# Another order for the opening of a fused state-space and MLP kernel: C's loads over two queues, later x and second weights, per-row products in place of wide ones

## The chip, the cores and the metric

The kernel runs on one core of a Trainium2 chip. The metric is the time of one execution in microseconds of the device; the kernel before took 336.55 us (median of three runs, 336.38 to 338.06). Engines are named as in the profile: PE (TensorE, its weight loads PEld), DVE (VectorE), ACT (ScalarE), POOL (GpSimd), SP (SyncE, which here only issues DMAs). ACT can issue DMAs too.

## The reference

A chunked state-space scan (Mamba-2) is followed by a two-layer MLP with a hard-swish in between. Inputs are x (4, 8, 768, 32), a (4, 8, 768), B and C (4, 8, 768, 16), and two weight matrices in float64, 256 x 2048 and 2048 x 256.

```python
log_a = np.log(np.clip(a, 1e-06, 1.0))
for c in range(nc):                          # chunks of 32 tokens
    cum = np.cumsum(la, axis=-1)
    L = np.exp(cum[:, :, :, None] - cum[:, :, None, :]) * causal
    CB = np.einsum('bhin,bhjn->bhij', Cc, Bc)
    y_intra = np.einsum('bhij,bhjd->bhid', CB * L, xc)
    y_inter = np.einsum('bhin,bhnd->bhid', Cc, state) * np.exp(cum)[:, :, :, None]
    y[:, :, sl] = y_intra + y_inter
    state = decay_full * state + np.sum(Bx, axis=2)
...
h = x @ w_in
g = h * np.clip(h + 3.0, 0.0, 6.0) / 6.0
return (g @ w_out).astype(np.float32)
```

## The kernel before

The kernel cuts the 768 tokens into NC = 6 chunks of P = 128 and each chunk into two halves of 64. The outer loop `for k in range(NC)` runs the MLP of chunk k while the scan of the next chunk is woven into it. Everything in front of that loop is the opening: it prepares constants, the scan of chunk 0 and part of chunk 1, and turns the first weights from float64 into float32. The order on every engine is the order in which the program writes the instructions (a manual schedule); the framework adds the waits.

The opening, in the names and lines that the change touches:

- Loads. `a` goes out on SP first (L83). `load_w(0, nc.scalar)` (L146) issues the first megabyte of weights on ACT, `load_bc(0)` issues C (as eight DMAs on SP, `pairs_first`, L99 to L106, one for each batch and parity of heads) and B (on ACT). `load_x(0)` and `load_w(1)` follow on SP. The activation table is loaded behind ACT's issues (L150).
- The decay matrix L. `log_a`, `add_up` (a scan) and `in_three` give the cumulative sums as three bfloat16 parts in `split`. PE builds the differences of every pair of tokens in PSUM: `diff_mask` (L355) writes the causal mask into eight banks, `mask_again` three of them once more, `diff_less` (L382) subtracts, `diff_pick` (L388) adds. `diff_pick` has two forms: 16 products of 64 columns for each batch with `pick`, or two wide ones with `of_batch` on rows that DVE has prepared in `spread_rows` (L277, two instructions). ACT takes the exponential (`diff_exp`, L404). `first_eto` (L409) makes the decay to each token.
- Products. `turn_b` transposes B on PE and copies it out of PSUM on ACT; `turn_squares` (L505) transposes C on DVE and `part_heads` (L511) splits it by head parity into `cT`. `scores` (L558) multiplies C and B into four banks `cb`, opens the banks of y (`own_banks`) and lets `into_state` (L581) multiply x with the decayed B (`ends`, on POOL). `multiply` (L608) copies the sums on ACT (`take`, L604, and two scalings to `mid`) and multiplies L with `cb` on DVE (L621). `mix` (L655) makes y from L and x (L667) and from the state (L545); `keep` (L676) copies y to `yT` on ACT, and `mlp_in` (L688) starts.
- Weights. `decode(i)` (L190) is a generator; `weights(i, n)` runs n of its steps. Its steps: a copy of the top 16 bits on ACT (L202) with the significand on DVE (L207, L211); exponent and sign masks on DVE (L221, L223); two relus on ACT (L227, L230); an OR and the last product on DVE (L234, L244). Three raw buffers hold the weights as loaded; `load_w(3)` uses the first again.
- Fillers. `diff_mask` contains 30 products of one column at its last batch of chunk 0 (L364), `busy` (L532) writes two products that nobody reads, and the last 18 of the 32 products of `mlp_in` are cut into two halves of 256 columns (L691).
- `renew(0)` (L638, DVE) makes the state after chunk 0, in `first_out`'s loop at (i, b) = (1, 0) (L1217).

The order of the opening is written out in L1137 to L1180.

## Time and profile before

| what | us |
| --- | --- |
| median of three runs | 336.55 |
| the profiled execution | 337.3 |
| its span | 335.6 |
| PE busy in the span | 327.6 |
| DVE, ACT, POOL busy | 264.2, 208.2, 130.3 |
| first product of `mlp_in` in the profile | 21.7 |

How to read it: the span is what the profiler covers, and the execution's own time has some more around it. A busy PE is not PE at its peak. A line of a timeline or chain gives the start in us from the span's start, the length, the engine, the line of the program and the operation, output before input. The chain of waits is followed back from the last instruction to whatever released each step; "issue" in it is time in which an engine waited for nothing that the profile shows.

## The change

Loads. The table load comes first on ACT. C's eight loads are cut by head, 32 partitions and four batches each, the even heads on ACT and the odd ones on SP. B and the first weights follow on SP. `load_x(0)` is called after the third `diff_exp` of chunk 0 and begins with a copy of one column into the tile on ACT, for which the DMA has to wait. `load_w(1)` is called behind the second step of `decode(0)` and begins with a memset on DVE.

Differences. `spread_rows`, `of_batch` and `of_head` go; every batch of both chunks takes the 16 products with `pick`. The masks are written by 18 products instead of 32; the 30 one-column products, `busy` and the halves in `mlp_in` go.

Order. C is turned and split right behind `in_three`. `turn_b(0)` copies on DVE for chunk 0. Chunk 1's batches 0 and 1 come ahead of the scores, 2 and 3 behind them; `own_banks` and `into_state` are calls of their own after the steps with the two relus. `renew(0)` moves up ahead of `mix(0)`. The second weights are decoded in one go by `decode_halves(1)` after `keep(0)`, with two halves of the columns in most of its steps.

```diff
@@ -98,6 +98,13 @@
 
         def pairs_first(src):
             t = loads.tile([P, 2, NB, 4, N], FP32, name="pairs", tag="bc")
+            if c == 0:
+                for h in range(NH):
+                    rows = slice(h // 2 * 32, h // 2 * 32 + 32)
+                    (nc.sync if h % 2 else nc.scalar).dma_start(
+                        out=t[rows, h % 2].rearrange("s b a n -> s b (a n)"),
+                        in_=src[:, h, sl, :].rearrange("b (s a) n -> s b (a n)", a=4))
+                return t
             for b in range(NB):
                 for h in range(2):
                     nc.sync.dma_start(
@@ -107,9 +114,11 @@
 
         if 0 < c < TURN:
             bcs[c] = [tokens_first(C, name="C", tag="bc")]
-        Bs[c] = tokens_first(B, nc.scalar if c == 0 else nc.sync, name="B", bufs=1)
         if c == 0:
-            bcs[c] = [pairs_first(C), Bs[c]]
+            bcs[c] = [pairs_first(C)]
+        Bs[c] = tokens_first(B, name="B", bufs=1)
+        if c == 0:
+            bcs[c].append(Bs[c])
         elif c < TURN:
             bcs[c].append(Bs[c])
         else:
@@ -118,6 +127,8 @@
     def load_x(c):
         sl = slice(c * P, (c + 1) * P)
         xts[c] = loads.tile([P, NB * NH, D], FP32, name="xt", bufs=1)
+        if c == 0:
+            nc.scalar.copy(out=xts[c][:, 0, :1], in_=bias_hi)
         nc.sync.dma_start(out=xts[c], in_=x[:, :, sl, :].rearrange("b h s d -> s (b h) d"))
 
     NP = 4
@@ -139,15 +150,13 @@
             src = moe_w_out[r0:r0 + FP * P, :].rearrange("(k p) m -> p k m", p=P)
             dst = raw.rearrange("p (k m) -> p k m", k=FP)
         raws[i] = raw
-        if i == 2:
+        if 0 < i < 3:
             nc.vector.memset(raw[:, :1], 0)
         queue.dma_start(out=dst, in_=src)
 
-    load_w(0, nc.scalar)
+    nc.scalar.preload_act_table_set("natural_log_exp_and_others")
     load_bc(0)
-    load_x(0)
-    load_w(1)
-    nc.scalar.preload_act_table_set("natural_log_exp_and_others")
+    load_w(0)
 
 
     ident = const.tile([P, P], FP32, name="ident")
@@ -187,6 +196,40 @@
         fill=0.0, base=N - 1, channel_multiplier=-1)
     parity = const.tile([P, 2], FP32, name="parity")
 
+    def decode_halves(i):
+
+        n, cut = NK * FP * P, FP * P // 2
+        top = raws[i].bitcast(U16).rearrange("p (k f w) -> p k f w", k=NK, w=4)[..., 3]
+        lo, hi = (raws[i].rearrange("p (n w) -> p n w", w=2)[:, :, w] for w in range(2))
+        s = att.tile([P, n], U16, name="ws").rearrange("p (k f) -> p k f", k=NK)
+        e = att.tile([P, n], U16, name="we").rearrange("p (k f) -> p k f", k=NK)
+        m = att.tile([P, n], U32, name="wm")
+        halves = [slice(h * cut, (h + 1) * cut) for h in range(2)]
+        for h in halves:
+            nc.scalar.copy(out=s[:, :, h], in_=top[:, :, h])
+        nc.vector.tensor_scalar(
+            out=m, in0=hi, scalar1=0xFFFFF, scalar2=0x100000,
+            op0=ALU.bitwise_and, op1=ALU.bitwise_or)
+        for h in halves:
+            for t, mask in ((e, 0x7FF0), (s, 0x8000)):
+                nc.vector.tensor_scalar(
+                    out=t[:, :, h], in0=s[:, :, h], scalar1=mask, scalar2=None,
+                    op0=ALU.bitwise_and)
+            nc.scalar.activation(
+                e[:, :, h].bitcast(BF16), e[:, :, h], AF.Relu, bias=bias_hi, scale=-8.0)
+            nc.scalar.activation(
+                e[:, :, h], e[:, :, h].bitcast(BF16), AF.Relu, bias=bias_lo, scale=-1.0)
+        nc.vector.scalar_tensor_tensor(
+            out=m.bitcast(FP32), in0=lo, scalar=2.0 ** -32, in1=m, op0=ALU.mult, op1=ALU.add)
+        load_w(i + NRAW)
+        m = m.bitcast(FP32).rearrange("p (k f) -> p k f", k=NK)
+        for h in halves:
+            nc.vector.tensor_tensor(
+                out=e[:, :, h], in0=e[:, :, h], in1=s[:, :, h], op=ALU.bitwise_or)
+            nc.vector.scalar_tensor_tensor(
+                out=w_in[i][:, :, h], in0=m[:, :, h], scalar=2.0 ** -20,
+                in1=e[:, :, h].bitcast(BF16), op0=ALU.mult, op1=ALU.mult)
+
     def decode(i):
 
 
@@ -198,10 +241,7 @@
         s = att.tile([P, n], U16, name="ws")
         e = att.tile([P, n], U16, name="we")
         m = att.tile([P, n], U32, name="wm")
-        for sl in (slice(0, n),) if i != 1 else (slice(0, n // 2), slice(n // 2, n)):
-            nc.scalar.copy(out=s[:, sl], in_=top[:, sl])
-            if i == 1 and sl.start == 0:
-                yield
+        nc.scalar.copy(out=s, in_=top)
 
         def significand():
             nc.vector.tensor_scalar(
@@ -222,13 +262,14 @@
             out=e, in0=s, scalar1=0x7FF0, scalar2=None, op0=ALU.bitwise_and)
         nc.vector.tensor_scalar(
             out=s, in0=s, scalar1=0x8000, scalar2=None, op0=ALU.bitwise_and)
-        next(parts_m, None)
+        if i:
+            next(parts_m)
         yield
         nc.scalar.activation(e.bitcast(BF16), e, AF.Relu, bias=bias_hi, scale=-8.0)
         next(parts_m, None)
         yield
         nc.scalar.activation(e, e.bitcast(BF16), AF.Relu, bias=bias_lo, scale=-1.0)
-        if i and i + NRAW < 2 * NP:
+        if i > 1 and i + NRAW < 2 * NP:
             load_w(i + NRAW)
         yield
         nc.vector.tensor_tensor(out=e, in0=e, in1=s, op=ALU.bitwise_or)
@@ -252,9 +293,6 @@
     picks = const.tile([P, G * N], BF16, name="picks")
     mid = pre[:G, 9].bitcast(BF16)[:, :2 * P]
     low = pre[:G, 10, :2 * P]
-    spread = [pre[:, 11 + c].bitcast(BF16).rearrange("k (h i) -> k h i", h=NH) for c in range(2)]
-    of_batch = const.tile([P, NB], BF16, name="of_batch")
-    of_head = const.tile([P, NH], BF16, name="of_head")
 
     cum_c = cum.rearrange("g (c p) -> g c p", p=P)
     ends_at = (slice(0, 2 * P), slice(2 * P, S))
@@ -264,21 +302,11 @@
             nc.vector.tensor_reduce(
                 out=pick, in_=ident[:, :pad].rearrange("g (r q) -> g q r", r=3), axis=AX.X,
                 op=ALU.add)
-            nc.vector.tensor_reduce(
-                out=of_batch, in_=pick.rearrange("k (b h) -> k b h", b=NB), axis=AX.X, op=ALU.add)
-            nc.vector.tensor_reduce(
-                out=of_head, in_=pick.rearrange("k (b h) -> k h b", b=NB), axis=AX.X, op=ALU.add)
         nc.scalar.mul(less, pick, -1.0)
         nc.gpsimd.tensor_copy(
             picks.rearrange("k (g n) -> k g n", n=N), pick.unsqueeze(2).to_broadcast([P, G, N]))
         nc.vector.tensor_reduce(
             out=parity, in_=head.rearrange("p q t -> p t q"), axis=AX.X, op=ALU.add)
-
-    def spread_rows(c):
-
-        nc.vector.tensor_tensor(
-            out=spread[c], in0=split[:, c].unsqueeze(1).to_broadcast([P, NH, P]),
-            in1=of_head.unsqueeze(2).to_broadcast([P, NH, P]), op=ALU.mult)
 
     def log_a(sl):
         nc.vector.tensor_scalar(
@@ -360,12 +388,7 @@
             d = ps_o.tile([P, NH, HT], FP32, name="d", tag="o")
         else:
             d = ps_y.tile([P, NH, HT], FP32, name="d", tag=f"y{b % 2}")
-        if (c, b) == (0, NB - 1):
-            for _ in range(30):
-                nc.tensor.matmul(
-                    out=d[:1, 0, :1], lhsT=ident_h[:, :1], rhs=hide[:, :1], start=True, stop=True,
-                    skip_group_check=True)
-        n = NH // 4
+        n = NH if c else NH // (2 if b == 0 else 4)
         for h in range(0, NH, n):
             nc.tensor.matmul(
                 out=d[:, h:h + n], lhsT=ident_h,
@@ -386,13 +409,6 @@
             start=False, stop=True, skip_group_check=True)
 
     def diff_pick(c, b):
-        if c or b >= 2:
-            for a, rows in enumerate(HALF):
-                nc.tensor.matmul(
-                    out=ds[c, b][rows], lhsT=of_batch[:, b:b + 1].to_broadcast([P, HT]),
-                    rhs=spread[c][:, :, rows], start=False, stop=True,
-                    tile_position=(0, a * HT), skip_group_check=True)
-            return
         for h in range(NH):
             for a, rows in enumerate(HALF):
                 g = b * NH + h
@@ -470,7 +486,7 @@
 
         t_ps = turn_ps(c, 1)
         transposes(c, 1, t_ps)
-        nc.scalar.copy(out=turned(c)[0], in_=t_ps)
+        (nc.scalar.copy if c else nc.vector.tensor_copy)(out=turned(c)[0], in_=t_ps)
 
     def turn_c(c, t_ps):
 
@@ -529,13 +545,6 @@
         part_heads(c)
         fade(c)
 
-    def busy(n, bank):
-
-        for _ in range(n):
-            nc.tensor.matmul(
-                out=bank[:, :256], lhsT=ident,
-                rhs=ident.unsqueeze(1).to_broadcast([P, 2, P]), start=True, stop=True)
-
     def from_state(c, a, pairs=range(NQ)):
 
         csT, state = bTs[c][2], (mids[c] if a else states[c - 1])
@@ -563,7 +572,7 @@
 
         bT, cT, _ = bTs[c]
         cbs[c] = [ps.tile([P, NB, 2, HT], FP32, name="cb", tag=f"f{q}") for q in range(NQ)]
-        if c not in ys:
+        if c not in ys and c:
             own_banks(c)
         for b in range(NB):
             for a, rows in enumerate(HALF):
@@ -575,7 +584,7 @@
                         tile_position=(32 * q, a * HT), skip_group_check=True)
         if c == TURN:
             from_state(c, 0)
-        if c <= TURN:
+        if 0 < c <= TURN:
             into_state(c, *range(1 if c == TURN else 2))
 
     def into_state(c, *halves):
@@ -688,7 +697,7 @@
     def mlp_in(k, f, between):
         h = ps.tile([P, TB], FP32, name="h", tag=f"f{f % 4}")
         for j in range(NK):
-            n = TB // (1 + (f * NK + j >= NF * NK - 18))
+            n = TB // (1 + (f * NK + j >= NF * NK - 0))
             for t in range(0, TB, n):
                 nc.tensor.matmul(
                     out=h[:, t:t + n], lhsT=w_in[f // FP][:, j, f % FP * P:(f % FP + 1) * P],
@@ -1144,38 +1153,40 @@
     in_three()
     for b in range(3):
         mask_again(0, b)
-    for c in range(2):
-        spread_rows(c)
-    diff(0, 0, 1)
-    diff(0, 2, 3)
-    weights(0, 1)
+    turn_squares(bcs[0][0], turned(0)[2])
+    part_heads(0)
+    for b in (0, 2):
+        diff(0, b, b + 1)
     for b in range(NB):
         diff_exp(0, b)
+        if b == 2:
+            load_x(0)
     first_eto()
-    diff(1, 2, 3)
+    turn_b(0)
+    diff(1, 0)
+    diff(1, 1)
     weights(0, 1)
     for b in range(NB):
         ends(0, b)
-    turn_b(0)
-    diff(1, 0, 1)
+    weights(0, 1)
+    load_w(1)
+    scores(0)
+    for b in range(2, NB):
+        diff(1, b)
+        diff_exp(1, b)
     weights(0, 2)
-    diff_exp(1, 2)
-    diff_exp(1, 3)
-    turn_squares(bcs[0][0], turned(0)[2])
-    part_heads(0)
+    own_banks(0)
+    into_state(0, 0, 1)
+    multiply(0)
     fade(0, HALF[1])
     weights(0, 1)
-    busy(2, ps.tile([P, NB * P], FP32, name="d", tag="f3"))
-    scores(0)
-    multiply(0)
+    weights(0, 1)
     load_w(2)
     load_w(3)
-    weights(0, 1)
-    weights(1, 1)
+    renew(0)
     mix(0)
-    keep(0, lambda: weights(1, 1))
-    weights(1, 3)
-    weights(1, 1)
+    keep(0)
+    decode_halves(1)
     load_bc(1)
     load_x(1)
 
@@ -1214,8 +1225,6 @@
                     first_out(b, i, c)
                     for n in w_more.get((i, b), ()):
                         next(ins[n])
-                    if (i, b) == (1, 0):
-                        renew(0)
                     if (i, b) == (1, 1):
                         by_token(cum_q)
                     if (i, b) == (2, 0):
```

## What I predicted, before the changed kernel had run

> **What bounds the kernel now.** I read the page first (busy times and slices), then the chain of waits of the first 50 us, then the timelines of PE, ACT and DVE before 24 us, then stretches of 1 us for the DMA.

> ```profile
> PE 327.6 (98%) x3361; PEld 272.8 (81%) x3361; DVE 264.2 (79%) x418; ACT 208.2 (62%) x448; POOL 130.3 (39%) x125
> ...
> 9.18 3.62 DMA pairs<-in_C_dram
> ...
> 12.98 1.12 DVE csT L507
> 14.13 0.89 DVE cT L517 x2
> 15.16 1.20 PE cb L572 x59
> 16.36 0.84 PE y L590 x50
> ...
> 17.22 0.38 ACT adds L606
> ...
> 17.64 0.90 PE y L667 x55
> 18.55 0.61 PE y L545 x16
> 19.16 0.26 PE y L667 x12
> 19.42 1.03 issue
> 20.44 0.75 PE y L667 x43
> 21.19 0.61 PE y L545 x16
> 21.80 27.75 PE h L693 x100
> ```

> The first line is the page's, the others are the chain: start, length, what. From 21.80 the chain is almost only TensorE, and over 49.5 to 335.6 PE is busy 282.4 of 286.1 us. So the change is worth what it does to the moment at which `mlp_in` starts (21.80). Before it the chain is: C's last load lands at 12.80, C is turned (L507), split by head parity (L517), multiplied with B (L572), the sums taken by ACT (L606), the mixing products (L667, L545), and in their midst PE stands 1.03 us for "issue", that is for nothing but its own instructions. From L667's start to `mlp_in` it is 21.80 - 17.64 = 4.16 us, 3.13 without that stall.

> ```profile
> 6.42 1.49 PE L378 MATMUL d<-hide,ident_h 128*128 128x512 bf16 x3
> 7.70 1.06 PE L383 MATMUL d<-less,split 128*128 128x512 bf16 x2
> 8.69 0.84 PE L399 MATMUL d<-split,pick 128*64 128x64 bf16 x32
> ...
> 12.93 1.15 ACT L227 ACTIVATE we<-we,bias_hi 128x1024 bf16<-128x1024 uint16 x1
> 14.11 1.15 ACT L230 ACTIVATE we<-we,bias_lo 128x1024 uint16<-128x1024 bf16 x1
> 15.17 1.07 ACT L407 ACTIVATE L<-d 128x512 f32<-128x512 f32 x2
> ```

> Timeline: start, length, instruction. PE takes 0.43 to 0.5 us for 512 columns up to about 8.6, then 0.026 us for 64 (32 in 0.84), twice as fast. ACT does its two relus of the first weights (2.3 us) in the shade of C's wait; that is the place to watch.

> **The profile's own time** is 337.3 us (span 335.6 and 1.7 around it), 0.75 over the median 336.55. I carry the change of `mlp_in`'s start to both.

> **Part 1, loads.** C was eight issues on SP, 1.25 to 9.75, held up in between (0.56 to 2.14 each). Now four go on SP and four on ACT, behind the table load (1.28, so 0.79 to 2.07). An issue costs ACT 0.47 to 0.49 by its own rows, up to 0.71 by SP's C rows: 1.9 to 2.8, I take 2.4. ACT is free at 4.5, not 3.08. Queued behind that are `less` (0.23) and the first logarithm, which started at 4.34: now about 4.7. DVE's scan and `in_three` wait for it, so `split` is whole at 7.5 instead of 7.23 (bounds 7.23 to 8.0).
> C lands between the last issue (4.5) + 2.6, the earliest C landing after its issue ended (a's: 1.19 to 3.8), and 4.5 + 3.62 = 8.1 by the chain's last C row. I take 7.5; DVE can use it from 7.5, and it costs nothing up to 10, since DVE then idles until 12.0.
> B follows on SP at about 4.0. Its packets took from 5.8 to 10.7 in the DMA records beside C's; a later B (issued 198.7) was down at 205. So it lands between 8 and 10.7, wanted at 11.1: nothing. The first weights, 6.0 us from issue to ACT's copy before, now come behind B: 10.7 to 13.4, wanted at 12.3. Even 13.4 only delays DVE's decode, which has 1 us in hand.

> **Part 2, TensorE and the first exponentials.** The masks are 18 instructions with the same 4096 columns, the 30 one-column products go, so PE is done with masks at about 6.9 and waits for `split`. `less` twice from 7.7 (1.06 by L383's row), picks from 8.69, as before, since PE itself held this back before. First exponential 9.3 (9.32). Batches 2 and 3 now have 32 picks (0.84) where four wide products took 0.62, so the four exponentials end at 11.75 plus the little copy that holds x (0.1 to 0.23): 11.9 against 11.53. In return DVE loses `spread_rows` (2.36) and two reductions (0.39), which is what lets it turn C at 7.5 to 8.7 and split it by 9.6.
> PE: `e_ps` at 10.85 (0.29), transposes of B to 11.75, DVE's new copy of `bT` 12.0 to 12.65 (0.59 by ACT's row, 0.68 by DVE's L621). PE next does chunk 1, batches 0 and 1 with picks, (0.22 + 0.42) x 2, to 13.05, then the scores, 1.2, to 14.25: 2.1 us earlier than before.

> **Part 3, what comes then on ACT.** After `eto` (to 12.3) and the copy of the sign halves (1.11, to 13.4) ACT's next instructions are the two exponentials of chunk 1, for which PE must first do another 0.65 each behind the scores: 15.2 to 16.3. Then the two relus, now uncovered, 1.17 each with their step: 18.65. Only behind them, in ACT's order, stands `take` (L606): 18.65 to 19.0. So L667 starts at 19.05 instead of 17.64. The two `mid` scalings (0.63) end at 19.65, before PE wants them (19.9).
> x is issued behind the third exponential, at 11.4 instead of 9.79. It took until 15.5 (5.7) before, 4.7 to 5.2 at 197.8 and 248.3: it lands at 16.1 to 17.1. The state products may start at 16.3, take 0.85, and are wanted at 18.6: up to 17.7 hidden.
> DVE: `wm` 12.65, then 0.69 + 1.23 + 0.64 + 0.52 to 15.7, L621's four (2.48) to 18.2, `fade` 0.42, the last two steps 0.68 + 1.22 to 20.6. All ahead of PE.

> **Sum.** L667 at 19.05 + 3.13 = 22.2 without the stall, 21.8 before: +0.4. The 1.03 gained is more than paid for by the 1.4 that ACT's relus cost.
> The stall: PE's instructions come in 16 KB pieces (26 pieces in the page's queue line); one piece ran at 18.50 for 0.97 us, just as the second weights' packets ended, and PE went on at 20.44. In the changed order that point lies in the first mixing half, the piece is asked for near 14.8, and the second weights, now issued behind DVE's sign step (15.7, 10.62 before), don't move before 17. I take no stall; 1.03 is the other end.

> **Part 4, second weights and after.** They land at about 20.0 (before: 18.7). ACT begins their copy when `keep` is done (22.5), and two halves of copy and relus (0.66 x 2, 0.6 x 4) end at 26.4; DVE finishes `w_in[1]` at 27.7 and the first `times_ramp` at 28.4. The fifth block reuses that bank at 22.2 + 6.87 = 29.1: hidden by 0.7 (1.7 before). If that is gone, each us late is a us on the path. `renew` (about 1 us of DVE) moves into the same stretch and is in these times; where it stood PE had no wait. Whole instead of halved products in `mlp_in`: 36 x 0.4295 against 72 x 0.2158, -0.1. PE's instructions up to its end are 517 either way (417 + 100, 453 + 64), so later pieces fall as before. Total +0.3 to +0.4.

> [...]

> **Rivals.** [...]
> [...]
> *The instruction stall stays* (another transfer stands before the piece): +1.0, **338.0**.
> *The loads don't do what they say:* C lands at 12.8 as before. Turning, splitting and the copy of `bT` are in DVE's order, scores start at 15.5, +2.5 more, **339.4**. Against: no weights run ahead of it now.
> *Faster by over 1.7:* L667 would have to start before 17.0, with the exponentials ending at 14.3; no row gives this.

> **Chances.** Forecast 0.34, earlier doubling 0.12, stall 0.12 (half of it beyond 338.2), slow PE 0.28, late loads 0.04, faster for a reason not seen here 0.10. A measurement of this kernel can tell about 0.5%, 1.7 us, from no change: same 0.34 + 0.12 + 0.06 = 0.52, slower 0.28 + 0.06 + 0.04 = 0.38, faster 0.10. Time 336.55 + 0.35 = 336.9. The likeliest case alone spans 336.2 to 337.9; with the others 335.3 to 339.0.

> **What would show it.** Right: L507 starts near 7.5, L572 near 13, L606 directly behind L230 near 18.6, L667 near 19, L693 near 22.2 and no "issue" between. Wrong: ACT's issues or L286 far later than 4.7; L399 at 0.05 us each after 8.7; L590 released by x's DMA after 17.7; waits of L693 for L801 or `w_in` between 28 and 36; L606 well ahead of L230.

## The result, and the profile after

| | before | after |
| --- | --- | --- |
| median of the runs side by side (us) | 336.98 (4 runs, 336.38 to 338.06) | 342.05 (4 runs, 341.87 to 342.62) |
| the profiled execution, its span | 337.3, 335.6 | 341.9, 340.2 |
| mean granted TensorE clock in the span | 1.000 | 0.983 |
| first mixing product (L667 / L676) | 17.64 | 17.30 |
| "issue" stall in the mixing | 1.03 | 3.10 |
| `mlp_in` begins, and its first stretch takes | 21.80, 27.75 | 24.83, 29.43 |

The change makes the kernel slower: ratio 1.015, 95% interval 1.0118 to 1.0181, outside the predicted range of 335.3 to 339.0. In what follows a ratio leaves out executions that stand over 1.5% above the fastest of the same kernel; where executions of one kernel fall into two groups, their single times are given.

The page of the changed kernel, its first line of busy times and the clock in 40 slices of 8.5 us:

```profile
PE 329.0 (97%) x3361; PEld 266.0 (78%) x3361; DVE 262.4 (77%) x420; ACT 208.5 (61%) x450; POOL 128.7 (38%) x125
...
PEclk9958999999999999999999999999999999999999
```

PE has the same 3361 products and is busy 1.4 us more. The new thing is in the second line: in the third slice, 17.0 to 25.5 us, TensorE was granted half its clock, after it had had the full one. The prediction has no term for that.

The chain of waits of the changed kernel (start, length, what):

```profile
16.99 0.27 ACT adds L615
17.25 0.04 issue
17.30 0.79 PE y L676 x49
18.09 3.10 issue
21.18 0.44 PE y L676 x8
21.62 1.04 PE y L554 x16
22.67 1.11 PE y L676 x61
23.78 1.04 PE y L554 x16
24.83 29.43 PE h L702 x64
```

Three things are to be seen. Mixing begins at 17.30, which is 0.34 *earlier* than before. After 56 products (49 of them on the chain) PE stops for 3.10 us with no wait that the profile shows ("issue"). And what follows is slow: L554's sixteen products take 1.04 us where before they took 0.61.

The stretches of 1 us of the changed kernel (stretch, its length, then each engine's busy share, granted clock, DMA share, GB/s):

```profile
16.00:17.00 1.00, 0.57 (x58) 0.41 (x34) 1.00 (x3) 1.00 (x2) 0.00 (x0) 1.00 0.89 209
17.00:18.00 1.00, 0.70 (x56) 0.63 (x57) 0.96 (x3) 0.77 (x3) 0.00 (x0) 1.00 0.91 377
18.00:19.00 1.00, 0.09 (x8) 0.00 (x0) 1.00 (x1) 0.00 (x0) 0.00 (x0) 0.55 0.90 360
19.00:20.00 1.00, 0.00 (x0) 0.00 (x0) 0.96 (x5) 0.00 (x0) 0.00 (x0) 0.50 0.10 41
...
28.00:29.00 1.00, 1.00 (x3) 0.39 (x2) 0.96 (x3) 0.97 (x2) 0.00 (x0) 0.83 0.05 16
```

The clock falls at 18.10, as the stall begins, and is back at 28.34. Its records have it full from 7.86 for 10.24 us, half for 10.24 and full again for 310.61; in the kernel before it is full from 9.07 for 327.68. These are 3, 3, 91 and 96 times 3.413 us, so stretches of 3.41 us are compared below. While PE has nothing to do, DMA is nine tenths busy until 19: these are the second weights' packets (15.57 to 19.39). In this window a piece of the queue that the page calls `instruction` moves (26 pieces, 0.43 MB, 16 KB each), seen in the DMA queues of 18.8 to 19.8 us:

```profile
q1 hardware_dynamic: 30, 0.07, 18.6%
q8 instruction: 1, 0.02, 5.9%
```

In the records this piece runs from 18.84 to 19.79, among the last of the weights' packets, and PE goes on at 21.18. In the kernel before it ran from 18.19 to 19.16 and PE went on at 20.44. That it carries instructions of PE is an estimate from these times: both stops end 1.28 and 1.39 us behind it. The piece is only 0.65 us later than before; but PE now comes to the place where it stops, taken here as the border between two pieces, at 18.09 instead of 19.42. There it had done 64 + 16 + 12 = 92 mixing products, here 56, as the timelines count them (the chain lists fewer, since not every product stands on it). 36 more of its products stand ahead of `mlp_in` (453 against 417), so the border, behind the 349th product of PE's program in both kernels, has moved up the mixing by those 36, and the piece has not moved with it. Of the 2.07 us that the stall grew, 1.33 are the earlier border and 0.74 the later going on.

**Where 4.7 us come from.** Mixing starts 0.34 earlier; the stall is 3.10 - 1.03 = 2.07 longer; the rest of the mixing takes 24.83 - 17.30 - 3.10 = 4.43 instead of 3.13, 1.30 more; `mlp_in` up to the next long chain piece takes 29.43 instead of 27.75, 1.68 more. The last agrees with 3.5 us (24.83 to 28.34) at half clock. -0.34 + 2.07 + 1.30 + 1.68 = +4.71; the span grew by 4.6. Behind 54 us the difference stays between 4.5 and 4.7. So 2.07 is the stall and about 3 the clock, and the opening that the change rearranged gives back 0.34.

The opening itself, from the timeline of the changed kernel (start, length, engine, instruction, in brackets the idle time before it and what ended it):

```profile
0.79 1.28 ACT L157 ACT_TABLE_LOAD   x1 [0.79 <-PEq L1380]
0.82 2.71 ACTq L104 DMA_DIRECT2D pairs<-in_C_dram  x4
...
6.61 1.08 DVE L523 STREAM_TRANSPOSE csT<-pairs 128x512 f32<-128x512 f32 x1
8.26 1.76 ACT L423 ACTIVATE L<-d 128x512 f32<-128x512 f32 x3 [3.63 <-PE d L415]
11.54 1.21 PE L581 MATMUL cb<-cT,bT 32*64 32x128 f32 x64
14.66 1.14 ACT L268 ACTIVATE we<-we,bias_hi 128x1024 bf16<-128x1024 uint16 x1
15.73 0.85 PE L599 MATMUL y<-xt,bs 64*32 64x64 f32 x64 [1.60 <-DMA xt<-in_x_dram]
15.84 1.15 ACT L271 ACTIVATE we<-we,bias_lo 128x1024 uint16<-128x1024 bf16 x1
16.89 0.35 ACT L615 COPY adds<-y 128x256 f32<-128x256 f32 x1
```

C is turned at 6.61, 6.4 us earlier than before, and the scores follow 3.6 us earlier; then L615 stands behind the two relus, and all but 0.34 of it is gone.

## The experiments

The profile leaves two readings open. **Packets:** the instruction piece waits behind the second weights' packets, and the stall, with it the slow clock, comes from that. **Clock:** the rearranged opening leaves PE too little work between 14 and 17 us (in the changed kernel PE is idle from 14.13 to 15.73), and the clock falls for that, stall or no stall. The runs set the one against the other, under names of their own: theories A, B and C, later R and M, are spelled out in the texts that stand before each result. A third reading, that ACT's sums come too late behind the relus, is set aside by the result, since the mixing begins earlier than before.

### Second weights behind the L times cb products

```
     multiply(0)
+    load_w(1)     # was ahead of scores(0)
```

> The changed kernel with one call moved: the second weights are loaded behind the four L times cb products on DVE (issue near 17 instead of 14.6 us). Theory A (two causes: the piece of PE's instructions is asked for near 15.8 and stands behind the second weights' packets, which gives the 3.1 us stall; and the clock is halved at 18.3 because of the thin PE work of the 3.4 us before it, whatever the stall does): the stall in the mixing products is gone, the clock still falls near 18.3, mlp_in starts near 21.5 and is some 1.5 us longer than 27.8; time 338 to 339.5. Theory B (one cause: the stall, which also cools the clock): no stall and the clock full throughout, mlp_in starts near 20.5; time 335.5 to 336.5. Theory C (the stall comes from the number of instructions and not from the transfer): still 3 us, time 341.5 to 342.5.

Measured: 340.57 us, ratio 1.0104 (1.0088 to 1.012). Theory A has the clock right and the stall wrong; B and C have neither. The chain of waits:

```profile
16.89 1.12 PE y L676 x54
18.01 1.66 issue
19.67 0.44 PE y L676 x8
...
23.31 29.45 PE h L702 x64
```

and its stretches, first the 3.41 us that end where the clock falls, then single us:

```profile
13.22:16.63 3.41, 1.25 (x80) 0.92 (x72) 3.38 (x7) 3.14 (x5) 0.00 (x0) 1.00 0.31 28
...
15.00:16.00 1.00, 0.42 (x42) 0.45 (x46) 1.00 (x3) 0.97 (x2) 0.00 (x0) 1.00 0.01 2
16.00:17.00 1.00, 0.54 (x47) 0.38 (x45) 1.00 (x4) 1.00 (x4) 0.00 (x0) 0.81 0.00 0
17.00:18.00 1.00, 1.00 (x56) 0.77 (x57) 0.96 (x3) 0.37 (x2) 0.00 (x0) 0.50 0.17 29
18.00:19.00 1.00, 0.01 (x1) 0.00 (x0) 1.00 (x1) 0.00 (x0) 0.00 (x0) 0.50 0.79 143
```

and the first of these stretches in the kernel before:

```profile
13.22:16.63 3.41, 2.70 (x103) 1.99 (x102) 3.00 (x6) 2.98 (x4) 0.01 (x1) 1.00 1.16 202
```

These rows tell the two apart. DMA is idle from 15 to 17, nothing stands before the piece (17.28 to 18.22 in the records; the weights' packets begin at 17.97), and the stall is 1.66 us instead of 3.10: that 1.4 goes to the packets. But the stall doesn't vanish, so the piece also begins late by itself. And the clock falls at 16.63, 1.4 us *before* PE stops: here the stall can't be what lowers it. In the 3.41 us before the fall PE was busy for 1.25, in the same stretch of the kernel before for 2.70. From 16.63 to 26.87 the granted clock is 0.50.

### Second weights with x

```
         if b == 2:
             load_x(0)
+            load_w(1)
```

> The changed kernel with the second weights issued directly behind x (near 10.6 instead of 14.6 us), so that their packets end some 1.5 us earlier (near 17.5 instead of 19.1). Theory A and B: PE goes on about 2.1 us after the last of those packets, as in both kernels so far (18.3 to 20.44, 19.1 to 21.18), so the stall shrinks from 3.1 to about 1.5; A has the clock fall near 18.3 all the same, time 339.5 to 341; B lets it stay full if the pause is short enough, time 337.5 to 338.5. Theory C: stall and time unchanged, 341.5 to 342.5.

Measured: 342.09 us, ratio 1.0144 (1.0114 to 1.0175), above what theories A and B had; C has the time but not the stall, which did shrink. The weights' packets run 14.61 to 18.42, as early as before the change (14.49 to 18.30), the piece comes at 17.95 among the last of them, and the stall is 2.17. So giving the weights their old time gives back only 0.9 of the stall, and again the clock falls first (17.30, stall at 17.95). PE goes on at 20.12, even 0.3 ahead of the kernel before; the stall is longer than its 1.03 because PE is at the border 1.5 us sooner.

### Filler products where PE was idle

```
+    zero = const.tile([P, P], BF16, name="zero")     # memset to 0
+    for _ in range(7):                               # ahead of weights(0, 2)
+        nc.tensor.matmul(out=cbs[0][3]..., lhsT=zero, rhs=ident_h..., start=False, ...)
```

> The changed kernel with seven products of a zero tile (512 columns each, added to the fourth cb bank) on PE between the last differences and the state products, where it waits 1.6 us for x. Second weights as in the changed kernel. Theory A: the clock doesn't fall near 18.3, since that window is now filled; the stall stays near 3 us and may itself cool the clock one window later, near 21.7; time 339 to 341.5, the lower end if it stays full. Theory B: stall and clock as in the changed kernel, 341.5 to 342.5. The state products start at most 0.2 us later than before.

Measured: 336.67, 343.78, 336.77 and 344.39 us, with a mean clock of 1.000 in the two short ones and about 0.985 in the others; before, 337.14 in the same set. Neither theory had the short ones (339 to 342.5). The chain of the profiled, short execution:

```profile
17.17 0.86 PE y L678 x53
18.03 0.61 PE y L556 x16
18.64 0.79 PE y L678 x53
19.43 0.61 PE y L556 x16
20.04 27.66 PE h L704 x64
```

No stall, full clock, and the mixing takes 2.87 us where `e1_w1_late` took 6.42 with a stall of 1.66 in it: 4.76, or 1.9 for the clock alone. The instruction piece now came at 14.70 to 15.75, ahead of the weights (15.38 on). So both losses are gone at once, and the run doesn't tell by itself which of them brings the other. What it does show is that seven products of no use are worth 5.2 us against the changed kernel, when they work. The two long executions were not profiled; that they miss the race between piece and packets is likely from `e12_m13_w1first_fill`, not shown. An estimate speaks for it: their mean clock is that of the changed kernel, where the slow clock cost about 3 us, and they are 7 us longer than the short ones, so about 4 are left for a stall.

It shows a second thing. `mlp_in` begins 1.76 earlier than in the kernel before, yet the span is only 0.6 shorter (335.0 against 335.6): 1.85 ahead at the end of `mlp_in` (47.70 against 49.55), 1.45 at 126, 0.6 at the end. The gain goes in parts: about 0.45 between 82 and 105 us, where the chain leaves PE for ACT and DVE at the splitting of weights (87 to 94.5) and the kernel before had PE alone, and about 0.3 near 176 and 0.4 near 223 us, at each of which the chain of `e3_fill` has a short "issue" (0.14 and 0.38).

### Both

> The fill of the run before and the late second weights together. Theory A: neither stall nor slow clock, mixing products at 17.3, mlp_in near 20.5 and 27.7 us long; time 335 to 336, that is 1 us under the kernel before. Theory B: the same as the late second weights alone. Theory C: 341 to 342.5.

With late weights and the filler: 340.98 us (338.68 to 341.88), ratio 1.0101 (1.0061 to 1.0141); theory A's 335 to 336 missed. With no weights in the way the piece still came only at 16.74, the stall was 1.63, and the clock fell at 19.71, 1.9 *after* the stall had begun this time. The filler thus keeps the clock up to the stall, but does not by itself bring the piece early; that it came at 14.70 in `e3_fill` and at 16.74 here, with the same products on PE, has no explanation in these runs. One difference is seen: at the border before this one PE had to stop for 0.23 us here (at 13.38), and not in `e3_fill`.

### The kernel before without its two products that nobody reads

```
-            busy(2, ...)
```

> The kernel before without its two products that nobody reads (busy, at 13.3 to 14.4 us). Theory A, now from the late second weights' run, where the clock was halved 1.1 us ahead of the stall: the clock falls where the PE work of some 3.4 us is thin. Without them PE works some 1.6 of the 3.4 us around 12.8 to 16.2, as in the changed kernel around 15 to 18.4, so the clock is halved for a part of the opening in most runs, mlp_in takes 1 to 2 us more and the time is 338.5 to 341. Theory B (only a stall cools it): no change, 336.5 to 338.

Measured: 337.28 us over ten runs, ratio 1.0014 (0.9995 to 1.0034). Theory A, by which the clock is halved for a part of the opening in most runs, missed: nine of the ten had a mean clock of 0.994 to 1.000, and one, of 340.04 us, 0.984. In the profiled execution, of 337.14, the clock was full and the stall 0.54 at 19.63, though PE was busy for only 1.68 of the 3.42 us from 13.17 to 16.59. So the two products of `busy`, which the change drops, are not what holds the clock in most executions of the kernel before. The thirty one-column products, which it drops too, were not taken out of that kernel by any run.

### The changed kernel with twenty one-column products

```
+        if (c, b) == (0, NB - 1):
+            for _ in range(20):
+                nc.tensor.matmul(out=d[:1, 0, :1], lhsT=ident_h[:, :1], rhs=hide[:, :1], ...)
```

> The changed kernel with 20 products of one column behind the masks, so that PE reaches the borders of its 16 KB instruction pieces 20 products earlier. Theory R (the piece that the mixing products need is asked for about 1 us behind the border before it, and loses a race with the second weights' packets by little): it is asked for near 12.9 and comes before them, no stall, and the clock alone is left: 338 to 339.5. Theory M (a piece that PE reaches before it is there costs a short stop, and the one behind it is then fetched only on demand, as the runs with late second weights look, where it began at 17.1 and 17.6 with nothing else moving): a stop of some 0.3 near 13 and a stall of 2 to 3 us in the mixing products; 340 to 342.5.

Measured: a median of 347.22 us over runs of 343.79 to 351.12, ratio 1.022 (1.0187 to 1.0254). Theory R missed. Of theory M the two stops came true and the time did not: with twenty products more ahead of it PE comes to the border twenty products earlier in its work, and it now stops twice, 0.38 at 12.73 and 2.80 at 18.18. The profile is that of the longest execution, whose clock falls again from 183 us on; its first fall is at 16.18, 2.0 before the second stop. With these products in place the clock falls as it does without them. Moving the border earlier by itself does not make the piece come earlier: it still came at 18.81, behind the weights.

### Masks in eight products, late weights, filler

```
-        n = NH if c else NH // (2 if b == 0 else 4)
+        n = NH
```

with the two edits of `e4_both`.

> The late second weights and the fill together, and the masks in 8 products instead of 18, so that the border that PE reached too early in those runs (13.4 to 13.6) lies behind the last differences. Theory M: no stop near 13.5, the next piece comes near 15, no stall, clock full: 335 to 336. Theory R: the same as this, since no packets stand before the piece. If the stall of 1.6 is still there, both fall, and the piece depends on something else; then 338.5 to 342.

Measured: a median of 338.68 us over ten runs (five of 336.98 to 337.87 with the full clock, five of 339.49 to 340.22 at 0.988 to 0.990), ratio 1.0045 (1.002 to 1.0071). In the profiled execution, of 337.49, the piece came at 14.41, there was no stall, and the clock stayed full from 8.04, as theories M and R had it; the 335 to 336 us that they had did not come. What is late now is the second weights, as its chain shows:

```profile
16.59 5.24 DMA raw<-in_moe_w_in_dram
21.85 1.25 ACT ws L211 x2
```

So the late load is a bound of its own once the stall is gone: this is why the weights can't simply be moved out of the piece's way.

### x at once

```
-            load_x(0)     # behind the third exponential, with ACT's hold
+    load_x(0)             # behind load_w(0)
```

> The changed kernel with x issued behind the first weights and not held behind the exponentials. The state products start near 14.8 instead of 15.7, since x is no longer what they wait for; the copy of the sums stands behind the two relus on ACT (17.0) all the same, and so do the mixing products (17.3). Theory A: the second weights and the thin stretch are as they were, so stall and halved clock stay: 341 to 342.5. If the hold of x is the cause: 337 to 338.5.

Measured: 342.73 us, ratio 1.0165 (1.0131 to 1.02). The time is close to theory A's; the stalls lie elsewhere than it had them. The chain:

```profile
13.40 2.11 issue
15.51 0.40 PE d L414 x5
...
19.05 1.12 PE y L675 x54
20.17 0.81 issue
```

With x moving early the *first* instruction piece is the late one (12.55 to 14.09, against 10.8 in the changed kernel), and the long stall lies there. The hold of x may do a good deed that the change's words don't name, to keep x's packets away from that piece, but this is argued and not shown: x's packets begin at 10.41 here and at 11.14 in the changed kernel, and in `e1_w1_late` they begin at 10.64 with the piece at 10.98. The sum is the same as in the changed kernel, 2.92 us of stalls against 3.10.

### Weights behind the first L times cb product, with and without filler

```
     for q in ...:          # in multiply
+        if c == 0 and q == 0:
+            load_w(1)          # was ahead of scores(0)
```

with masks in eight products; `e9` with ten filler products, `e10` without.

> The changed kernel with the masks in 8 products, the second weights issued behind the first of the four L times cb products (near 15.3, 0.7 later than in the changed kernel), seven products of a zero tile before the state products and three behind them: 517 instructions of TensorE up to the end of mlp_in, as in both kernels. What the runs so far say (the instruction piece that the mixing products need must come before the second weights' packets; thin PE work halves the clock; second weights issued at 17 come too late for the fifth block): the piece comes near 14.8, no stall, second weights land near 20.5, clock full in most executions, mlp_in at 20.0 to 20.3: 336.0 to 337.0, 0 to 1 us under the kernel before; an execution in which the clock is halved all the same takes 339 to 340.

Measured: 336.37, 342.98, 342.36, 343.64, 336.2 and 342.53 us. The two with the full clock give 0.9981 (0.9958 to 1.0004) of the time before: no stall there, the piece at 14.30, `mlp_in` from 19.98. The others are longer by 6, at a clock of 0.984 to 0.990; expected were 336 to 337 in most executions and 339 to 340 in the rest.

> The same without the ten filling products. If thin PE work alone halves the clock, there is no stall, but the clock falls between 15 and 19 in all or nearly all executions; the second mixing half and mlp_in are slower by 2.5 to 3.5 us together: 338.5 to 340.5. If it was the stall that kept it down, 336 to 337 as with the fill.

Measured: 342.54 us, ratio 1.0165 (1.0145 to 1.0186), a miss: the border before this one was moved behind the wait for x (16.0), the piece still came at 19.14, and the stall was 2.94.

### The border moved by five products

```
-        n = NH if c else NH // (2 if b == 0 else 4)
+        n = NH if c or b == 0 else NH // (2 if b < 3 else 4)
```

with the weights as in `e10`; `e12` has the ten filler products too.

> The run without fill showed the border of the instruction piece crossed only in the state products (16.3), behind x's wait, so that the piece came after the second weights again. Here the masks are 13 products: the border lies in the last differences, some 5 products later than in the changed kernel and before x's wait; second weights at the first L times cb product, no fill. Race theory: the piece begins near 15, ahead of the second weights' packets (16), no stall in the mixing products. Clock theory (thin PE work by itself): it falls near 16 to 19 in all or nearly all executions, and 338.5 to 340.5 is measured. If there is no stall and the clock stays full, 336 to 337, the stall is the one cause.

Measured: 342.84 us, ratio 1.018 (1.0165 to 1.0195), a miss: stall 2.87, the piece at 18.60, clock down at 17.60, 0.5 ahead of the stall.

> The same with the seven and the three filling products. The border is crossed ahead of the fill, earlier than in the run with 8 mask products (14.6), so that the race is won in more executions: 336.0 to 337.0 where the clock stays full, 338.5 to 340 where it falls for two windows, and no execution at 342 or above, which the stall alone explains.

Measured over twelve runs: 335.79, 336.46 and 336.78 us with the full clock, one of 340.37, and eight of 343.17 to 345.11; median 343.63. It missed too: the race isn't won more often. The profiled execution is a long one; its stretches, the first the 3.41 us that end where its clock falls:

```profile
16.52:19.93 3.41, 1.20 (x54) 0.71 (x52) 3.12 (x8) 0.63 (x3) 0.00 (x0) 1.00 0.80 286
...
18.00:19.00 1.00, 0.00 (x0) 0.00 (x0) 1.00 (x3) 0.00 (x0) 0.00 (x0) 1.00 0.95 389
...
20.00:21.00 1.00, 0.00 (x0) 0.00 (x0) 0.69 (x1) 0.00 (x0) 0.00 (x0) 0.50 0.96 188
```

Here the order is plainly the other way round. PE had been kept busy (3.22 of the 3.41 us up to 16.52), its clock is full when it stops at 17.71, it waits 1.4 us, with DMA nine tenths busy, for a piece that comes at 19.10, and only at 19.93 does the clock fall, when the stall has made a stretch of 3.41 us with PE busy for 1.20. So this long execution needed no slack opening: the late piece brought the stall (3.71), and the clock fell 2.2 us into it.

**What the runs show together.** The stall and the clock are two losses. The stall comes without a clock fall ahead of it (`e12_m13_w1first_fill`, `e4_both`; in the kernel before 1.03 with no fall at all). The clock falls ahead of the stall wherever PE's idle time at 14 to 16 us was left unfilled and the fall could be dated apart from it (by 1.4, 0.65, 2.0, 0.7 and 0.5 us in `e1`, `e2`, `e6`, `e10`, `e11`; in the changed kernel itself the two begin within 0.01 us). So both readings are right, each for its part, and one measure nearly joins them: PE's busy time in the 3.41 us that end at the fall.

| | PE busy of 3.41 us |
| --- | --- |
| up to the fall: after, `e1`, `e2`, `e6`, `e10`, `e11` | 1.64, 1.25, 1.19, 1.87, 1.63, 1.34 |
| up to the fall, a stall within: `e4`, `e8`, `e12` | 1.22, 1.39, 1.20 |
| least between 9 and 28 us, no fall: before, `e5`, `e3`, `e7`, `e9` | 1.92, 1.67, 2.69, 2.71, 3.35 |

By this measure it makes no difference whether the gap is a slack opening or the stall. But the two groups overlap: with 1.87 the clock fell in `e6`, with 1.67 it held in `e5`. So no bound can be read, busy time alone doesn't decide, and the kernel before, where it held, has 1.92 in its least stretch, the one around its stall of 1.03.

No profiled execution had the fall without any stall, so its price alone is read within executions (4.76 against 2.87 to 3.13 for the mixing, 29.3 to 30.2 against 27.7 for `mlp_in`), not from a time.

No variant beats the kernel before in its median. The shortest executions, 335.8 to 336.4 us, are within 0.4% of it.

## Why the prediction was wrong

**The step that failed** is the stall in the sum: "I take no stall; 1.03 is the other end", because "the piece is asked for near 14.8, and the second weights ... don't move before 17". The weights moved from 15.57, and the piece came at 18.84, behind nearly all of them; the stall that I took as nothing was 3.10. Their issue was put behind DVE's sign step, which I had at 15.7; it ended at 14.51, so the weights came ahead too. But a piece that starts at 14.8 would still have gone ahead of packets that begin at 15.57, as it did in `e3_fill` (14.70 against 15.38). The start of the piece is what failed first: I moved it up along with the border, which does stand in the first mixing half as the prediction says, and `e1_w1_late` shows that with DMA idle the piece still began at 17.28 only. Why it is so late stays open. And the other end was not 1.03: that row came from a kernel in which PE reached the border at 19.42 (and the piece ran from 18.19, not 18.50), and I had moved the border up by 36 products without adding them to the open wait. The rival that kept the stall had a part of the mechanism, "another transfer stands before the piece", and a third of the size; by `e1_w1_late` 1.4 of the 3.10 us go to that transfer.

**The second miss** is the clock. I asked only when it would first double, and gave chances to a late doubling (0.28) and to an earlier one (0.12). No run shows the late one; it doubled earlier than before: 32 picks in 0.72 us from 7.75, full from 7.86 by the clock's records (9.07 before). What I left out is that it can fall again in the middle of the work, here for 10.24 us at a cost of about 3: I counted PE's pauses as free where other work hides them, its wait for x among them ("up to 17.7 hidden"). That is right for time, as the wait of 1.60 us cost nothing on the path. For the clock it is not shown: PE was busy for 1.64 of the 3.41 us before the fall.

The half-clock spells are 10.24 us in six profiles, 6.83 in one and 13.65 in two: three, two and four times 3.41. In the 3.41 us before a fall PE was busy for 1.19 to 1.87 us in all nine profiles.

**Point by point, the rest.**
- C's loads: right that C is no bound any more. ACT was free at 3.53, not 4.5: the four issues (0.82 to 3.53) ran beside the table load (0.79 to 2.07), where I had them behind it. `split`, foreseen at 7.5, was whole at 6.59, the first exponential at 8.26 (9.3 foreseen).
- B, the first weights and x hidden: right for the first two. x wanted at 18.6 and to be down by 17.1; PE waited for it 1.60 us until 15.73, but the sums on ACT behind the relus were still later, so it cost nothing on the path.
- "Only behind them, in ACT's order, stands `take`": right. L615 is directly behind L271, at 16.89 instead of 18.65, as the whole opening was 1.75 ahead.
- The earlier doubling, to which I gave 0.12: it happened; together with ACT's earlier issues it is worth 1.75 at the start of the mixing (17.30 against 19.05 foreseen).
- The whole products in `mlp_in`, the second weights' deadline, 517 instructions: nothing seen to the contrary. Behind 54 us the difference stays at 4.5 to 4.7.

So the parts that I worked out in most detail were wrong by 1.75 us in the kernel's favour, and two things that the first trace shows only as one row and as a flat line of nines were wrong by 5 the other way.

## What to carry to other kernels

The place behind PE's 349th product, where it stood for 1.03 us before and for 3.10 after, has a due time, like a buffer: find such a place by the "issue" pieces of the chain, and ask of each bulk transfer whether it will stand before the next instruction piece (1.4 us here, by `e1_w1_late`). Price an opened gap on the engine that sets the end twice, once as time and once for the clock of what follows (about 3 us here). When something is moved up, move up everything that hangs on it in your sums too: the opening came 1.75 us early, and the transfer that I had counted as out of the way came early with it.

## What the hardware showed unexpectedly

- A piece of 16 KB for which PE stands takes 0.94 to 1.54 us in the records, and PE goes on 1.2 to 1.6 us behind its end, in every profile with such a stall. The border of the mixing lies behind the 349th product of PE's program in each of them (the 350th in `e12`), whatever the products are. The stop there took 1.03 us before and 3.10 after the change, and 1.66 in `e1_w1_late`, where no other packets moved when the piece began.
- What sets the start of the piece is open. It came at 14.3 to 14.7 in `e3`, `e7` and `e9`, at 16.7 to 17.3 with nothing in its way in `e4` and `e1`. Neither the place of the border (`e6`, `e10`, `e11`) nor the filler alone (`e4`, `e12`) decides it. Theory M has it late where PE had to stop at the border before, which `e4` (0.23), `e6` (0.38) and `e8` (2.11) bear out; but without such a stop it was late too, in the changed kernel, `e11` and `e12`.
- The same kernel with fillers has executions of 336 and of 343 us. Four executions of such a kernel can mislead: two of the four of `e3_fill` alone would make it equal to the kernel before.
- DMA issues in ACT's program ran while ACT loaded its table: 0.82 to 3.53 beside 0.79 to 2.07.
